# Spreading softmax weights over channels by a TensorE matrix instead of DMAs, and an earlier load of k, in a fused kernel of local attention and a state-space convolution

## The chip, the cores and the metric

The kernel runs on one core of a Trainium2 chip. The metric is device time in microseconds of one execution, and lower is better. The core has five engines that work side by side, each through its own instructions in order: TensorE (matmuls, PE in the profile), VectorE (DVE), ScalarE (ACT), GpSimd (POOL) and SyncE (SP), whose queue issues most DMAs. GpSimd's queue issues the rest. TensorE writes into PSUM, from where ScalarE moves results into on-chip memory ("evicts" them).

## The reference

Two independent halves share one output, side by side in the channels. All arrays are bf16, S = 2048 tokens, D = 576 channels.

```
# half A: 32 heads of 18 channels; a token looks at itself and 7 earlier ones, 2 apart
q, k, v = split(x @ wqkv)                                  # wqkv: 576 x 1728
logits[h, s, w] = sum_d q[h, s, d] * k[h, s - 2w, d] / sqrt(18)     # -1e9 where s - 2w < 0
attn = softmax(logits over w)
a = concat_heads(sum_w attn[h, s, w] * v[h, s - 2w, :]) @ wo        # wo: 576 x 576

# half B: a short convolution, a gate, a convolution as long as the sequence, a gate
k_shift[s, d] = sum_t k[s - 3 + t, d] * shift_k[d, 3 - t]           # 4 taps
kv = k_shift * v
y[s, d] = sum_{r <= s} kv[r, d] * ssm_k[d, s - r] + kv[s, d] * ssm_D[d]
b = q * y
out = concat([a, b], channels)
```

## The kernel before

**Order of work.** Nothing is issued where it is written. Each step is given to `Plan` by `op(engine, us, function, reads, writes, ...)`, with an engine letter (P TensorE, D VectorE, A ScalarE, G GpSimd, S SyncE), an assumed duration and the regions of buffers that it touches. `Plan.emit` sorts all steps once: for each engine it takes, among the steps that could begin earliest by the assumed durations, the one with the longest chain behind it (VectorE keeps close to the written order). The program then issues its instructions in that order, and every engine works through its own list strictly in order. So a changed step or a changed region can move instructions of other engines. PSUM is cut into four slots of two banks; a step with `opens` takes a slot and a later one with `closes` gives it back.

**Half A.** x is loaded by quarters of 512 tokens (`load_x`, `turn_x`) and turned by TensorE (`transpose_x`, `transpose_tail`) so that channels lie on partitions; quarters 2 and 3 are turned mostly by a transposing DMA. `project(comp, ct, jj)` computes q (comp 0), k (1) or v (2) for 128 channels and 1024 tokens: matmuls on L492 and L497, eviction on L516. `logits(hh)` takes one half hh of the tokens: VectorE multiplies q by four shifted views of k (L707, two product buffers), and TensorE adds the channels of each head by 0/1 matrices E into 32-row blocks j of 256 tokens (L717); ten products make a half, and after five of them ScalarE evicts a logits sum. `softmax(hh)` works on `attn[hh]`, 128 rows (4 token blocks of 32 heads) by 8 window positions by 256 tokens; its last step is the normalising multiply on L755.

To weigh v, the weights of a head must stand on all partitions of its channels. Each half has three chunks: c = 0 and c = 1 are two token blocks each with the 512 channels of ct 0 to 3, and c = 2 is all four blocks with the last 64 channels. `spread(n)` copies the 32 rows of a block to 64 partitions, each row to two neighbours, twice (four DMAs of 256 KB), into the buffer that `XB` names: chunks 0 and 3 share `tabk`, 1 and 5 share the start of `qk`, 4 has `qk` from 4096, 2 has `pv`. `weigh(n)` multiplies that buffer by shifted v on VectorE (L797, 128x4096; four products in a chunk c < 2, one in c = 2; three product buffers, `PB`), TensorE adds the eight window positions (L817, or L836 for c = 2), and ScalarE evicts into `pv` (L824). `output` multiplies by wo in sixteen groups (L869 and L872).

**Half B.** `taps(i)` computes k_shift and kv for a quarter of the tokens on VectorE (L569, L572, L579: eight instructions of 128x2304), from buffers that `load_k(i)` and `load_v(i)` fill. The kernel's shift weights come in as one row and are spread over the partitions by TensorE and ScalarE (`weight_rows`). The long convolution is done by tables of cosines and sines: `filter_spectrum` (ps_fk) for the filter and `x_spectrum` (ps_fx) for kv, both on L591 and L592 with evictions on L605; `partners` and `turn_filter` combine halves by accumulating DMAs from GpSimd's queue. In the last stage VectorE multiplies spectra (`products`, L941), TensorE adds them (`sums`, ps_z, L968) and transforms back (`inverse`, ps_inv, L1001), and `gate` multiplies by q and stores.

The early loads are given to the plan in this order:

```
    load_x(0)
    load_w(0, wv[:, 0], [r_w(0)])
    load_x(1)
    load_k(0)
    load_w(1, wv[:, 1], [r_w(1)])
    load_v(0)
    turn_x(0)
    load_k(1)
    load_v(1)
```

## Time and profile before

| | |
|---|---|
| median of 3 runs | 249.74 us (248.18 to 251.2) |
| the profiled execution | 249.37 us, of it 247.7 us span |
| busy: TensorE, VectorE | 203.3 us (82%), 201.0 us (81%) |
| busy: ScalarE, GpSimd | 136.2 us (55%), 45.4 us (18%) |
| moved by DMA | 40.74 MB, mean 164 GB/s |

The span is the time from the first to the last instruction of the profiled execution. Two engines are busy for four fifths of it, so an average names no bound; the stages have to be read one by one. A timeline row gives the start, the busy time, the engine, the line, and the operation with its output and inputs; a bracket says how long the engine had been idle before it and which work ended that wait. Some matmul records can be missing from a trace.

### The profile page before, as it was taken

The numbers are of one execution on the slowest core, as the hardware profiler recorded it, in microseconds if no ns is written. First come the engines' busy times: TensorE is split into PE (matmuls) and PEld (weight loads), VectorE is DVE, ScalarE is ACT, GpSimd is POOL, SyncE is SP. The second block draws the span as 40 slices with busy tenths as digits, with TensorE's granted clock in tenths as the row PEclk, the third lists the DMA queues.
The fourth block names the chain that finished last, engine by engine and source line by source line (L and its number), as shares of the span: only waits on it lengthen the run. The fifth ranks groups of instructions, "written<-read, shape, count | busy, mean of one in ns | idle before, by whom it ended". The sixth has DMA issues, their size and how long they took to land.

```text
span 247.7 us, 4427 instructions
## 1 busy us (share of the span) xinstructions
PE 203.3 (82%) x1838; PEld 102.9 (42%) x1845; DVE 201.0 (81%) x144; ACT 136.2 (55%) x186; POOL 45.4 (18%) x74
## 2 busy tenths in 40 slices
PE   4889989979999999996984399267499999956962
PEld 2453334323465533344642146023245566623532
DVE  7179999999986999999999300487999999999941
ACT  5843454696698963869991123015159756632351
POOL 7600030052404241174280000000001010010000
PEclk9999999999999999999999569957999999999798
DMA  6999969999913989999999999916301627473041
GB/s 208 333 278 293 372 125 283 221 220 160 127 24 44 156 107 173 188 230 218 194 194 199 204 180 198 228 70 171 118 0 50 145 46 195 146 181 108 3 145 46
DMA packets 36772, 40.74 MB, mean 164 GB/s; under 512 B 17264, under 2 KB 30448, under 8 KB 36752
## 3 DMA queue, kind: packets, MB, share of 16 engines
q1 hardware_dynamic: 26784, 26.81, 41.1%
q0 software_dynamic: 9968, 13.65, 35.0%
q8 instruction: 14, 0.23, 0.4%
q14 instruction: 6, 0.05, 0.1%
HBM read 13.11 MB, written 4.72 MB: 72 GB/s over the span
## 4 chain that ended last, share of the span: by engine, by line
PE 44%; DMA 17%; DVE 17%; issue 10%; ACT 7%; SPq 3%; POOL 0%; DVEq 0%; ACTq 0%; POOLq 0%
PE ps_proj L492 13%; PE ps_z L968 7%; PE ps_inv L1001 6%; DMA xw<-xw 6%; DVE big L707 5%; DMA pv<-big 4%; DMA tabk<-big 4%; PE ps_wo L869 4%; SPq L773 3%; DVE qk L941 3%; PE ps_fk L591 3%; DMA qk<-in_A_wo_dram 3%; PE ps_acc L817 2%; PE ps_proj L497 2%; DVE qk L797 2%
## 5 line engine op out<-in xcount | busy, mean ns | idle before, releaser
L492 PE MATMUL ps_proj<-xw 128*128 128x512 bf16 x185 | 46.4, 391 | 2.8 <-ACT qk L516 1.8
L707 DVE TENSOR_TENSOR big<-qk 128x4096 bf16<-128x4096 bf16 (+1 forms) x20 | 40.3, 2073 | 4.0 <-PE ps_log L717 3.4
L941 DVE TENSOR_TENSOR qk<-xw,Ks 128x3072 bf16<-128x3072 bf16 x18 | 30.9, 1750 | 0.0
L817 PE MATMUL ps_acc<-big,ident 64*64 64x512 bf16 x192 | 19.7, 442 | 12.9 <-DVE big L797 10.7
L492 PEld LDWEIGHTS <-xw 128*128 128x128 bf16 x192 | 17.5, 99 | 26.8 <-issue 9.5
L797 DVE TENSOR_TENSOR big<-tabk,big 128x4096 bf16<-128x4096 bf16 x6 | 13.6, 2287 | 16.9 <-DMA tabk<-big 15.8
L975 ACT ACTIVATE ab<-ps_z 128x768 bf16<-128x768 f32 x24 | 18.9, 808 | 13.3 <-PE ps_z L968 13.2
L824 ACT ACTIVATE pv<-ps_acc 128x1024 bf16<-128x1024 f32 x8 | 8.2, 1023 | 30.6 <-PE ps_acc L817 30.6
L516 ACT ACTIVATE qk<-ps_proj 128x1024 bf16<-128x1024 f32 x16 | 15.7, 1024 | 14.5 <-PE ps_proj L497 14.5
L869 PE MATMUL ps_wo<-qk,pv 128*128 128x288 bf16 x128 | 19.9, 302 | 1.1 <-ACT pv L824 1.1
L941 DVE TENSOR_TENSOR big<-xw,Ks 128x3072 bf16<-128x3072 bf16 x12 | 20.7, 1749 | 0.0
L605 ACT ACTIVATE Ks<-ps_fk 128x576 bf16<-128x576 f32 x32 | 18.8, 654 | 2.7 <-PE ps_fk L592 2.1
L817 PEld LDWEIGHTS <-ident 64*64 64x64 bf16 x256 | 9.3, 117 | 26.4 <-issue 16.3
L968 PE MATMUL ps_z<-qk,ident 64*64 64x384 bf16 x192 | 16.8, 339 | 3.5 <-DVE qk L941 3.4
L985 POOL DMA_DIRECT2D ab<-ab x3 | 3.6, 1196 | 85.6 <-ACT ab L975 85.6
L1001 PE MATMUL ps_inv<-ab,TI 128*128 128x288 bf16 (+2 forms) x128 | 18.2, 293 | 0.9 <-ACT ab L975 0.9
L605 ACT ACTIVATE xw<-ps_fx 128x576 bf16<-128x576 f32 x32 | 18.1, 679 | 0.9 <-PE ps_fx L592 0.9
L389 POOL DMA_DIRECT2D pv<-Ks x16 | 9.8, 616 | 44.8 <-DVE ab L572 24.3
L591 PE MATMUL ps_fk<-pv,tabk 128*128 128x384 bf16 x64 | 16.8, 328 | 0.2 <-ACT Ks L605 0.2
L572 DVE TENSOR_TENSOR ab<-ab,big 128x2304 bf16<-128x2304 bf16 x12 | 16.3, 1358 | 0.4
L591 PE MATMUL ps_fx<-ab,T 128*128 128x384 bf16 x64 | 16.6, 326 | 0.0
L569 DVE TENSOR_TENSOR big<-big 128x2304 bf16<-128x2304 bf16 x12 | 16.3, 1355 | 0.3
(120 smaller groups left out, 369.4 us busy)
## 6 DMA issues: line engine op xcount, KB each, us to landing
Ks<-Ks POOLq DMA_DIRECT2D x10, 576.0 KB, 10.1
qk<-big SPq DMA_DIRECT2D x12, 256.0 KB, 9.0
big<-in_B_k_dram SPq DMA_DIRECT2D x3, 1008.0 KB, 5.7
big<-in_B_v_dram SPq DMA_DIRECT2D x4, 576.0 KB, 10.0
pv<-Ks POOLq DMA_DIRECT2D x16, 144.0 KB, 8.0
xw<-xw POOLq DMA_DIRECT2D x4, 576.0 KB, 13.6
out_dram<-qk SPq DMA_DIRECT2D x8, 288.0 KB, 4.1
tabk<-big SPq DMA_DIRECT2D x8, 256.0 KB, 9.3
```

The lines of the kernel that those rows point to most:

```text
L492: nc.tensor.matmul(banks[key][:, jp, :], wq(kb, comp, 128 * ct, 128), xT(kb, 1024 * jj + 512 * jp, 512), start=(kb == 0), stop=False)
L569: nc.vector.tensor_tensor(o, kj[:, 3 - j:7 - j, :], skb[:, j, :].unsqueeze(1).to_broadcast([128, 4, D]), ALU.mult)
L591: nc.tensor.matmul(o[:, 0:2, :], w, rhs[:, 0:2, :], start=start, stop=stop, skip_group_check=True)
L605: nc.scalar.activation(dst(step), acc3(banks[key]), ACT.Copy, scale=scale * (1.0 if step else -2.0))
L707: nc.vector.tensor_tensor(view(prod, 0, [[m, 4], [1, m]]), view(t, oq, [[0, 4], [1, m]]), view(tk, oo + 2 + 8 * ug, [[2, 4], [1, m]]), ALU ...
L797: op("D", tt_us(4096), lambda: nc.vector.tensor_tensor(view(P, 0, [[2048, 2], [256, W], [1, 256]]), view(X, xo, [[2048, 2], [256, W], [1, ...
L817: nc.tensor.matmul(acc[64 * o:64 * o + 64, h, :], ident[64 * h:64 * h + 64, 64 * h:64 * h + 64], view(P, 256 * u, [[2048, 2], [1, 256]])[6 ...
L869: nc.tensor.matmul(ps[:, r, 0:HD], oT(hh, j + 2 * r, t)[:, o:o + 128], wo[:, t // 2, t % 2, HD * h:HD * h + HD], start=(t == 0), stop=False)
L941: op("D", 1.752, lambda: nc.vector.tensor_tensor(pr, view(xw, i * SPB + 4 * TH * t, [[4 * D, 2], [0, 2], [1, 4 * TH]]), view(Ks, (3 - j + ...
L968: nc.tensor.matmul(z[o:o + 64, h, 0:2 * TH], w[64 * h:64 * h + 64, 64 * h:64 * h + 64], pr[64 * h:64 * h + 64, part, cs, 2 * TH * q:2 * TH ...
L975: nc.scalar.activation(view(y_at(n, 1 - q, t, TH), 0, [[2 * D, 2], [D, 2], [1, TH]]), view(banks[key], 0, [[512, 2], [TH, 2], [1, TH]]), A ...
L1001: nc.tensor.matmul(ps[:, c, 0:w], TI[:, s // 2, s % 2, 2 * c + par, :], Yall[:, n % 2, par, s // 2, s % 2, c0:c0 + w], start=(s == 0), sto ...
```

## The change

Chunks with c < 2 (0, 1, 3 and 4) are no longer spread by DMAs. A new 0/1 matrix `rep` is built on GpSimd by eight selects: in each block of 32 rows, row h has ones in columns 2h, 2h + 1, 64 + 2h and 65 + 2h. For each quarter u of a chunk's 2048 columns, two matmuls of 32 rows take the two blocks into the two banks of a PSUM slot (`ps_rep`), and ScalarE evicts both at once (128x1024) into the same buffer that the DMAs filled. Chunks 2 and 5 keep their DMAs. k(0) is loaded second, w(0), x(1) and v(0) follow, and k(1) comes ahead of the transposing load. All four transposed pieces of x are evicted by ScalarE; VectorE had two. In `taps`, a multiply names to the plan only the four of seven rows of k that it reads.

```
+    rep = main.tile([128, 128], BF16, name="rep")
+    for j in range(4):
+        e = rep[32 * j:32 * j + 32, :].rearrange("p (e c) -> p e c", e=2)
+        nc.gpsimd.affine_select(e, ones128[32 * j:32 * j + 32, :].rearrange("p (e c) -> p e c", e=2),
+                                pattern=[[0, 2], [1, 64]], compare_op=ALU.is_ge, fill=0.0, base=0, channel_multiplier=-2)
+        nc.gpsimd.affine_select(e, e, pattern=[[0, 2], [-1, 64]], compare_op=ALU.is_ge, fill=0.0, base=1,
+                                channel_multiplier=2)
...
     load_x(0)
+    load_k(0)
     load_w(0, wv[:, 0], [r_w(0)])
     load_x(1)
-    load_k(0)
+    load_v(0)
     load_w(1, wv[:, 1], [r_w(1)])
-    load_v(0)
+    load_k(1)
     turn_x(0)
-    load_k(1)
     load_v(1)
...
-        transpose_x(0, kb, "A" if kb else "D")
+        transpose_x(0, kb, "A")
...
-        transpose_x(1, kb, "A" if kb else "D")
+        transpose_x(1, kb, "A")
...
-            op("D", 1.35, partial(mul, o, j), r=[rk, rw], w=[w], chain=True)
+            op("D", 1.35, partial(mul, o, j), r=[reg("big", o_kj[i % 2] + D * (3 - j), 4 * D), rw], w=[w], chain=True)
...
     def spread(n):
         hh, c = chunks[n]
         t, name, o = XB[n]
+        if c < 2:
+            for u in range(4):
+                key = ("rep", n, u)
+                own = reg("rep", 4 * n + u, 1)
+
+                def mm(u=u, key=key):
+                    ps = bank2(key, "ps_rep")
+                    for jj in range(2):
+                        j = 2 * c + jj
+                        nc.tensor.matmul(ps[:, jj, :], rep[32 * j:32 * j + 32, :],
+                                         attn[hh][32 * j:32 * j + 32, 2 * u:2 * u + 2, :], start=True, stop=True,
+                                         tile_position=(32 * j, 0))
+                op("P", 0.25, mm, r=[reg("big", AT[hh], 2048)], w=[own], opens=key, mode="s")
+                op("A", 1.02, lambda u=u, key=key: nc.scalar.activation(view(t, o + 512 * u, [[2048, 2], [1, 512]]),
+                                                                        banks[key][:], ACT.Copy),
+                   r=[own], w=[reg(name, o + 512 * u, 512), reg(name, o + 2048 + 512 * u, 512)], closes=key)
+            return
```

The plan also orders other work anew. Three places on ScalarE, whose list says what TensorE hands over and when, show it. In all, a row is a line of the kernel, the operation, its output and input, and how many stand in a row.

First, ScalarE at the first logits of half 0, before (L516 and L523 projections, L605 filter spectrum, L724 a logits sum, L748 the exponential):

```order
L523 ACTIVATE qk<-ps_proj 128x512 x2
L516 ACTIVATE big<-ps_proj 128x1024 x3
L605 ACTIVATE Ks<-ps_fk 128x3x192 x8
L724 ACTIVATE big<-ps_log 128x1024
L605 ACTIVATE Ks<-ps_fk 128x3x192 x18
L724 ACTIVATE big<-ps_log 128x1024
L605 ACTIVATE Ks<-ps_fk 128x3x192 x5
L748 ACTIVATE big<-big 128x2048
```

and now (the same operations, seven lines further down in the file):

```order
L530 ACTIVATE qk<-ps_proj 128x512 x2
L523 ACTIVATE big<-ps_proj 128x1024 x2
L612 ACTIVATE Ks<-ps_fk 128x3x192 x2
L523 ACTIVATE big<-ps_proj 128x1024
L612 ACTIVATE Ks<-ps_fk 128x3x192
L731 ACTIVATE big<-ps_log 128x1024
L612 ACTIVATE Ks<-ps_fk 128x3x192 x15
L731 ACTIVATE big<-ps_log 128x1024
L612 ACTIVATE Ks<-ps_fk 128x3x192 x5
L755 ACTIVATE big<-big 128x2048
```

Eight filter evictions, and the matmuls that feed them, moved from ahead of the second logits sum to behind it.

Second, ScalarE from the softmax of half 1 to chunk 2, before (L748 the exponential, L605 the spectrum of kv, L824 and L840 the weighed sums, L876 the output projection):

```order
L748 ACTIVATE big<-big 128x2048
L605 ACTIVATE xw<-ps_fx 128x3x192 x4
L824 ACTIVATE pv<-ps_acc 128x1024
L605 ACTIVATE xw<-ps_fx 128x3x192 x15
L824 ACTIVATE pv<-ps_acc 128x1024 x3
L840 ACTIVATE pv<-ps_acc 128x512
L876 ACTIVATE qk<-ps_wo 128x2x288 x4
```

and now (L789 is the new eviction, into the buffers of chunks 3 and 4; L849 and L865 are the weighed sums):

```order
L755 ACTIVATE big<-big 128x2048
L523 ACTIVATE big<-ps_proj 128x1024
L612 ACTIVATE xw<-ps_fx 128x3x192 x3
L849 ACTIVATE pv<-ps_acc 128x1024
L612 ACTIVATE xw<-ps_fx 128x3x192 x4
L530 ACTIVATE big<-ps_proj 128x512
L612 ACTIVATE xw<-ps_fx 128x3x192
L789 ACTIVATE tabk<-ps_rep 128x2x512 x4
L789 ACTIVATE qk<-ps_rep 128x2x512 x4
L849 ACTIVATE pv<-ps_acc 128x1024
L612 ACTIVATE xw<-ps_fx 128x3x192 x6
L849 ACTIVATE pv<-ps_acc 128x1024 x2
```

The spectrum of kv, which was nearly done here, is now split, and most of it stands behind the eight new evictions.

Third, ScalarE at the end of the weighing, before (L975 is the last stage's first sum):

```order
L876 ACTIVATE qk<-ps_wo 128x2x288 x4
L824 ACTIVATE pv<-ps_acc 128x1024
L876 ACTIVATE qk<-ps_wo 128x2x288 x4
L824 ACTIVATE pv<-ps_acc 128x1024 x3
L840 ACTIVATE pv<-ps_acc 128x512
L975 ACTIVATE ab<-ps_z 128x4x192
```

and now (L901 is the output projection, L1000 the last stage's first sum):

```order
L612 ACTIVATE xw<-ps_fx 128x3x192 x7
L849 ACTIVATE pv<-ps_acc 128x1024
L612 ACTIVATE xw<-ps_fx 128x3x192 x5
L849 ACTIVATE pv<-ps_acc 128x1024
L612 ACTIVATE xw<-ps_fx 128x3x192 x5
L849 ACTIVATE pv<-ps_acc 128x1024
L612 ACTIVATE xw<-ps_fx 128x3x192
L901 ACTIVATE qk<-ps_wo 128x2x288 x2
L849 ACTIVATE pv<-ps_acc 128x1024
L865 ACTIVATE pv<-ps_acc 128x512
L1000 ACTIVATE ab<-ps_z 128x4x192
```

Two groups of the output projection stand ahead of the last stage, where there were eight, and the other fourteen come inside it.

## Rows read from the trace of the kernel before

**Rows 1.** Stretches: length, busy PE PEld DVE ACT POOL (count), clock, DMA share, GB/s

```profile
0.00:14.27 14.27, 10.12 (x61) 5.79 (x62) 6.12 (x16) 9.11 (x12) 9.24 (x33) 1.00 0.88 277
...
96.50:109.78 13.28, 12.70 (x108) 5.29 (x107) 13.28 (x9) 8.66 (x13) 3.31 (x6) 1.00 1.03 200
109.78:128.90 19.12, 16.73 (x170) 10.80 (x170) 18.35 (x16) 17.59 (x28) 9.57 (x9) 1.00 1.14 207
128.90:158.20 29.30, 18.37 (x142) 9.31 (x139) 8.99 (x4) 6.27 (x8) 1.34 (x1) 0.83 1.07 196
158.20:181.20 23.00, 13.42 (x139) 6.09 (x139) 20.11 (x10) 5.61 (x8) 0.00 (x0) 0.78 0.43 128
181.20:216.00 34.80, 34.74 (x436) 20.49 (x440) 34.19 (x21) 24.43 (x36) 2.39 (x2) 1.00 0.40 101
216.00:231.00 15.00, 9.65 (x144) 5.55 (x140) 15.00 (x10) 4.89 (x7) 1.20 (x1) 0.93 0.51 126
```

**Rows 2.** VectorE's timeline: the taps, the logits' wait, the products, the last stage

```profile
14.27 1.35 DVE L569 TENSOR_TENSOR ab<-big 128x2304 bf16<-128x2304 bf16 x1
...
58.05 6.70 DVE L707 TENSOR_TENSOR big<-qk 128x4096 bf16<-128x4096 bf16 x3
...
76.56 7.83 DVE L707 TENSOR_TENSOR big<-qk 128x4096 bf16<-128x4096 bf16 x4 [2.61 <-PE ps_log L717]
...
128.91 2.29 DVE L797 TENSOR_TENSOR qk<-qk,big 128x4096 bf16<-128x4096 bf16 x1 [0.50 <-PE ps_acc L817]
...
140.09 2.29 DVE L797 TENSOR_TENSOR qk<-pv,big 128x4096 bf16<-128x4096 bf16 x1 [4.49 <-DMA pv<-big]
158.20 4.49 DVE L797 TENSOR_TENSOR big<-tabk,big 128x4096 bf16<-128x4096 bf16 x2 [15.81 <-DMA tabk<-big]
...
166.00 2.29 DVE L797 TENSOR_TENSOR big<-tabk,big 128x4096 bf16<-128x4096 bf16 x1 [1.10 <-PE ps_acc L817]
...
172.24 2.29 DVE L797 TENSOR_TENSOR qk<-qk,big 128x4096 bf16<-128x4096 bf16 x1 [1.75 <-PE ps_acc L817]
...
181.18 3.42 DVE L941 TENSOR_TENSOR qk<-xw,Ks 128x3072 bf16<-128x3072 bf16 x2
```

**Rows 3.** TensorE's timeline, single places

```profile
5.31 1.89 PE L455 MATMUL ps_x<-ident,Ks 128*128 128x128 bf16 x16 [0.87 <-DMA Ks<-in_A_x_dram]
...
9.18 3.59 PE L492 MATMUL ps_proj<-xw 128*128 128x512 bf16 x8
...
17.13 0.39 PE L497 MATMUL ps_proj<-xw 64*128 64x512 bf16 x2
...
37.47 0.42 PE L475 MATMUL ps_x<-ident,Ks 128*64 128x128 bf16 x8 [1.12 <-ACT TI L558]
37.83 1.90 PE L492 MATMUL ps_proj<-xw 128*128 128x512 bf16 x8
...
76.87 0.34 PE L591 MATMUL ps_fk<-pv,tabk 128*128 128x384 bf16 x1
...
77.12 0.33 PE L591 MATMUL ps_fk<-pv,tabk 128*128 128x384 bf16 x1
...
117.30 1.92 PE L817 MATMUL ps_acc<-big,ident 64*64 64x512 bf16 x32 [2.26 <-ACT xw L605]
...
148.97 1.15 PE L869 MATMUL ps_wo<-qk,pv 128*128 128x288 bf16 x8
...
150.28 1.15 PE L869 MATMUL ps_wo<-qk,pv 128*128 128x288 bf16 x8
```

**Rows 4.** SyncE's DMA queue: start and time of issue, two of the spreads

```profile
124.03 7.19 SPq L773 DMA_DIRECT2D pv<-big  x4
...
141.12 9.70 SPq L773 DMA_DIRECT2D tabk<-big  x4
```

**Rows 5.** DMA issues, part 6 of the page: count, KB each, median us to landing

```profile
pv<-big SPq DMA_DIRECT2D x4, 256.0 KB, 10.3
```

**Rows 6.** Part 5 of the page: busy, mean ns, idle before and what ended it

```profile
L516 ACT ACTIVATE qk<-ps_proj 128x1024 bf16<-128x1024 f32 x16 | 15.7, 1024 | 14.5 <-PE ps_proj L497 14.5
```

More of the change, by code (lines that the diff above doesn't have):

```diff
@@ L563, in taps @@
         kj, vt, kv = kjs[i % 2], vts[i % 2], ab[:, i]
-        rk, rv, rw, rt = (reg("big", o_kj[i % 2], 7 * D), reg("big", o_vt[i % 2], 4 * D), reg("big", o_skb, 4 * D),
+        rv, rw, rt = (reg("big", o_vt[i % 2], 4 * D), reg("big", o_skb, 4 * D),
                           reg("big", o_tB, 4 * D))
@@ L771, in fn @@
                 for e in range(2):
-                    j = 2 * c + jj if c < 2 else jj + 2 * e
+                    j = jj + 2 * e
                     nc.sync.dma_start(view(t, o + 2048 * jj, [[1, 2048]])[64 * e:64 * e + 64],
```

## The prediction

> **What bounds the kernel now.** I read the table of stretches first, then VectorE's timeline for the waits inside them, then TensorE and the DMA queue where those waits end. All times are of one execution: span 247.7 us, 249.37 us as timed, so 1.7 us lie outside the span; the median of the three runs shown is 249.74 us, so this execution stands for it within 0.2%.
>
> The table of stretches [rows 1] shows VectorE full from 96.50 to 128.9 us and again from 181.2 to 231 us. Between 128.9 and 158.2 it works 8.99 of 29.30 us, ScalarE 6.27, TensorE 18.37, while the DMA engines are at 1.07: there the kernel waits for copies. VectorE's timeline names them [rows 2]: the product of chunk 2 waits 4.49 us for the DMA into pv, that of chunk 3 waits 15.81 us for the DMA into tabk. Both are `spread`; the queue issues the one into tabk only at 141.12 [rows 4], behind the others, and all of them run beside the accumulating DMAs of `partners` and `turn_filter`. Three shorter waits, 0.50, 1.10 and 1.75 us, are for TensorE to give a product buffer back. Together that is 23.65 us of VectorE standing still between 109.78 and 181.18. Before 109.78 the one large wait is 2.61 us at 76.56, for a logits sum of TensorE. From 181.2 to 216 TensorE (34.74 of 34.80 us) and VectorE (34.19) are both full, so this last stage has no room for more TensorE work; from 216 on TensorE has 15.00 - 9.65 = 5.35 us free.
>
> **Early loads (first term).** k's three DMAs (by their shapes 128x2304, 112x1728 and 15x1728 in bf16: 1.03 MB) move ahead of the first weights (128x2304 and two of 64x576: 0.74 MB) and the second x. x(0) had landed when the first transposes ran at 5.31 [rows 3]; at 277 GB/s, the rate of the first stretch [rows 1], k is there 3.7 us later, at about 9.0. The other operand, the broadcast shift kernel, is ready earlier, since ScalarE's early work is not moved. So VectorE begins its convolution taps at 9.0 to 9.5 and not at 14.27 [rows 2], and as these run without a gap up to 58.05, they end at about 53. The two copies that VectorE gives to ScalarE stood in its idle time before the taps.
>
> That lead is not all kept, because the logits need TensorE. The weights now land after k: 9.0 + 0.74 MB at the same rate, 11.7, against projections that began at 9.18 [rows 3], so TensorE starts 2.5 us later. It gets 1.7 us of that back: the second inverse table is transposed in the idle time at the start, so its sixteen matmuls (eight of the size take 0.42 us, so 0.6 to 0.8; I take 0.6) and the wait of 1.12 us behind them at 37.47 [rows 3] vanish there. TensorE is 0.8 us late. But the written order changes in VectorE's favour: up to the second logits eviction ScalarE has 18 filter evictions and no longer 26. One drains four matmuls, a pair of them takes 0.25 us from start to start (76.87 to 77.12, [rows 3]), so 8 x 2 x 0.25 = 4.0 us of TensorE work go behind the logits instead of in front of them. The wait at 76.56 is for exactly these, so VectorE is 4.0 - 0.8 = 3.2 us earlier. **-3.2**; the ends are 0 (TensorE's late start is never made up) and -5.3 (the whole lead is kept). The later loads of k(1) and v(1) bear on no term: k(1) is now issued ahead of the transposing load, and v(1) is first needed after fifteen taps of 1.4 us, at about 30, some 10 us after its issue. The eight selects on GpSimd that build `rep` delay its later DMAs by a few us; what these bring is first read after 58.
>
> **Chunks 0 and 1 on TensorE and ScalarE (second term).** A pair of row-tiled matmuls of 512 columns takes 0.39 us (17.13, [rows 3]), so 16 pairs cost 6.2 us; if the two halves did not run side by side, 12.5. An eviction of 128x1024 takes 1.02 us [rows 6], 16 of them 16.4 us on ScalarE. The first eight run from VectorE's softmax 0 to the first product, where in the trace ScalarE is busy 8.66 of 13.28 us [rows 1]. The eight transform evictions that stood there go behind them, so 8.2 us fit. They hide behind the last logits products; they would stand on the path if all four PSUM slots were theirs when a logits sum wants one. **+0.5**, from 0 to +2.
>
> **The products (third term).** From 109.78 to 128.9 nothing but 0.5 us waited, so up to there the shift of -2.7 holds. Then 13 products are left at 2.2 us (two take 4.49, [rows 2]). Without any wait the last stage would begin at 181.18 - 23.65 - 2.7 = 154.8. What waits remain? Chunk 2 is still a DMA, issued behind softmax 1 at 124.03 [rows 4], now at 121.3. Before, its product started 16 us after; at the 10.3 us of one such copy [rows 5] with its three fellows issued in 2.5 us it would be 12.8, an estimate. It lands at 134 to 137; VectorE gets there at 133.5 (128.91 - 0.5 - 2.7, three products, and 1.2 us that the next sentences count): 2 us. Chunks 3 and 4 must first let chunk 0's last product read tabk; then eight evictions take 8.2 us, from about 123.5 to 131.7, long before chunk 3 is wanted at 138. But they fill ScalarE's queue and the PSUM slots, and the sum of chunk 1's first pair (1.9 us for 32 matmuls, as at 117.30 [rows 3]) comes late by about 1.2 us for the third buffer. Behind that ScalarE has 24 transform evictions between sums, and TensorE up to 28 transform matmuls (3.5 us) in front of a sum, where a pair of products takes 4.4 us: I count 0.9 us at chunk 3, and 1.1 us for what I cannot see. Together 5.2 of the 23.65 us: **-18.5**. The ends are -23.65 (no wait left) and -11 (the wait for chunk 2 is what it was, 4.5 us, and TensorE costs another 8).
>
> **The last stage (fourth term).** Before, eight of the sixteen groups of the output projection ran in the holes up to 181; now two do, and six go into the last stage. A group is 1.31 us (from 148.97 to the next at 150.28, [rows 3]), 7.9 us in all. By the order one of them comes before the point that was 216 us, five behind it, against 5.35 us free there: 1.3 + 6.6 - 5.35 = 2.5. The clock granted in that part was 0.93 [rows 1], after idle time, and fuller work could give some back; I count nothing. **+2.5**, from 0 to +7.9.
>
> **A rule against this.** What rows show: one pair of matmuls is 0.39 us and its eviction 1.02 [rows 3, 6]. The Trainium skill, TensorEngine Tiling (Array Packing), section PSUM Bottleneck, says that tiling speeds up TensorE but not the emptying of PSUM, which may then become the bottleneck. By that rule the evictions set the pace of the replication; it is the slower rival below, and the trace so far speaks against it only by ScalarE's idle time after 128.9.
>
> **Sum.** 249.37 - 3.2 + 0.5 - 18.5 + 2.5 = 230.7, against the median 231.
>
> **Rivals.**
> - The middle becomes TensorE's. From 96.50 to 181.2 it works 12.70 + 16.73 + 18.37 + 13.42 = 61.2 us [rows 1]. In the new order this stretch loses six output groups (7.9) and gains the 16 pairs (6.2 to 12.5) and 26 projection matmuls that the logits overtook (26 x 0.23 = 6.0; eight take 1.90 at 37.83, [rows 3]). That is 65.5 to 71.8 us, some of it at the low clock (0.83 and 0.78 there), which continuous work would shed, where the forecast leaves 66.7 us, from 96.50 - 3.2 to 181.18 - 2.7 - 18.5. At 71.8 plus 3 us of hand-overs the stage starts at 168: 239. For it: TensorE is then about as full as VectorE. Against: half of the work is independent of VectorE and fills gaps. Chance 0.2.
> - Nothing waits: all of 23.65 and 5.3 come, the last stage absorbs its groups: 249.37 - 28.95 = 220.4, with the 0.5 about 221. Chance 0.1.
> - The change does not do what it says: the copies into pv are late because of the accumulating DMAs, not of one another, and chunk 2 still comes at 140. Ten products (22 us) and 2 us of buffers follow: the stage starts at 164, and 249.37 - 17.2 + 2.5 = 234.7. It lies within the forecast's own spread; chance 0.15.
> - Slower: the sixteen evictions sit in ScalarE's strict order ahead of the sums, hold all four PSUM slots, and TensorE and then VectorE stop for each: 16 x (1.02 + 0.39) = 22.6 us on the path for 20.3 us of DMA waits removed, with all six groups added: 249.37 - 3.2 - 20.3 + 22.6 + 7.9 = 256.4. It decides from the point where each replication holds VectorE more than (20.3 + 3.2 - 7.9) / 16 = 1.0 us. For it: ScalarE is busy 17.59 of 19.12 us from 109.78 to 128.9 [rows 1]. Against: chunk 3's evictions end 6 us before their product. Chance 0.04.
>
> **How the numbers follow.** The forecast, 231, has 0.5, and 0.01 is left for what none of these names. The likeliest case alone reaches from 225 to 236 by the ends of its second and fourth terms and half the span of the third. Held 8 times in 10, the range takes in the TensorE rival and most of the no-wait one: 222 to 240. A difference under 1% is about what a measurement of this kernel cannot tell from none. Slower by over 1% is the last rival, 0.04; within 1% (247 to 252) needs a TensorE-bound middle and a lost lead together, 0.03; faster by over 1% is the rest, 0.93.
>
> **What would show it.** In the new profile: the first tap before 10 us; the first wait of VectorE among the logits shorter or gone at about 73; no DMA behind any wait but chunk 2's; VectorE's first spectrum product near 160; TensorE's free time after the first third of the last stage gone. The prediction is wrong if ScalarE runs unbroken between softmax 1 and chunk 3 with TensorE idle, if TensorE's clock falls in the middle, or if the last stage grows by more than 5 us over its 66.5.

## The result and the profile after

The changed kernel takes 228.34 us (median of 4 runs, 226.37 to 231.04) beside 248.96 us for the kernel before, measured with it (4 runs, 247.75 to 251.2): a ratio of 0.9136, with a 95% interval of 0.9026 to 0.9245. Here and below, ratios and their intervals leave out runs in a slower state, over 1.5% above the fastest of the same kernel, while medians and ranges count every run. The forecast was 231.0 in a range of 222 to 240. The profiled execution took 227.69 us, its span is 226.0 us, 21.7 less than before.

VectorE's timeline of the changed kernel, the rows that answer to [rows 2] (start, length, what it does, and in brackets the idle time before it and who ended it). Line numbers are 7 higher than before, behind `spread` 25:

```profile
9.00 1.36 DVE L576 TENSOR_TENSOR ab<-big 128x2304 bf16<-128x2304 bf16 x1 [3.13 <-DMA big<-in_B_k_dram]
...
30.06 1.36 DVE L586 TENSOR_TENSOR ab<-ab,big 128x2304 bf16<-128x2304 bf16 x1 [0.49 <-DMA big<-in_B_v_dram]
32.44 1.36 DVE L576 TENSOR_TENSOR ab<-big 128x2304 bf16<-128x2304 bf16 x1 [1.03 <-DMA big<-in_B_k_dram]
...
54.46 4.49 DVE L714 TENSOR_TENSOR big<-qk 128x4096 bf16<-128x4096 bf16 x2
61.09 5.81 DVE L714 TENSOR_TENSOR big<-qk 128x4096 bf16<-128x4096 bf16 x3 [2.13 <-PE ps_log L724]
...
72.88 7.83 DVE L714 TENSOR_TENSOR big<-qk 128x4096 bf16<-128x4096 bf16 x4 [0.73 <-PE ps_log L724]
...
106.99 1.23 DVE L714 TENSOR_TENSOR big<-qk 128x2048 bf16<-128x2048 bf16 x1 [1.45 <-PE ps_log L724]
...
109.20 2.29 DVE L822 TENSOR_TENSOR big<-tabk,big 128x4096 bf16<-128x4096 bf16 x1 [0.98 <-DMA qk<-in_A_wo_dram]
...
130.55 2.29 DVE L822 TENSOR_TENSOR qk<-qk,big 128x4096 bf16<-128x4096 bf16 x1 [2.50 <-PE ps_acc L842]
...
139.90 4.50 DVE L822 TENSOR_TENSOR big<-tabk,big 128x4096 bf16<-128x4096 bf16 x2 [0.45 <-ACT pv L849]
...
146.96 2.29 DVE L822 TENSOR_TENSOR big<-tabk,big 128x4096 bf16<-128x4096 bf16 x1 [0.36 <-PE ps_acc L842]
...
160.31 3.43 DVE L966 TENSOR_TENSOR qk<-xw,Ks 128x3072 bf16<-128x3072 bf16 x2
```

Read it against [rows 2]: the taps start 5.27 us earlier and end 3.6 us earlier (54.46, before 58.05), the logits' product that stood at 76.56 only 3.7, chunk 0's first product only 0.6 (109.20, before 109.78), and the last stage 20.9. The products wait for no DMA any more: of 23.65 us of standing still 3.31 are left. The wait at 109.20 is put down to a weight DMA; a logits sum of TensorE ended at 109.0 and VectorE went on at once, so I count it to that, like the 1.45 us before it. SyncE's queue, with [rows 4], issues chunk 2's copies in 3.07 us instead of 7.19:

```profile
123.73 3.07 SPq L798 DMA_DIRECT2D pv<-big  x4
...
137.28 4.91 SPq L798 DMA_DIRECT2D qk<-big  x4
```

The table of stretches of the changed kernel, with the columns of [rows 1] (the last row is the whole last stage):

```profile
93.16:109.20 16.04, 14.60 (x95) 4.03 (x95) 13.54 (x9) 11.43 (x13) 7.39 (x9) 0.79 1.16 177
109.20:130.55 21.35, 17.93 (x149) 8.44 (x150) 18.46 (x15) 15.53 (x19) 6.35 (x5) 0.92 0.64 119
130.55:144.30 13.75, 12.54 (x127) 7.26 (x128) 13.30 (x6) 12.28 (x18) 0.00 (x0) 1.00 1.07 198
144.30:160.31 16.01, 16.01 (x195) 9.17 (x196) 15.62 (x9) 12.48 (x20) 4.34 (x3) 1.00 0.82 161
...
160.31:195.10 34.79, 34.79 (x434) 20.20 (x430) 34.45 (x21) 23.99 (x35) 2.39 (x2) 1.00 0.53 125
195.10:210.10 15.00, 15.00 (x206) 8.63 (x201) 14.88 (x10) 8.40 (x13) 1.20 (x1) 1.00 0.60 162
210.10:226.00 15.90, 10.34 (x140) 6.30 (x128) 7.93 (x8) 6.56 (x10) 0.00 (x0) 1.00 0.28 94
160.31:226.00 65.69, 60.13 (x764) 35.12 (x756) 57.26 (x37) 38.95 (x56) 3.59 (x3) 1.00 0.49 126
```

TensorE (first figure behind the length) has no free time from 144 to 210 us. The last stage of the kernel before, as one row and its end behind [rows 1]:

```profile
231.00:247.70 16.70, 9.91 (x128) 6.10 (x120) 7.86 (x8) 5.57 (x8) 0.00 (x0) 0.91 0.21 72
181.18:247.70 66.52, 54.31 (x696) 32.14 (x696) 57.06 (x37) 34.92 (x50) 3.59 (x3) 0.96 0.38 99
```

So the stage holds 5.8 us more of busy TensorE and is 0.8 us shorter: TensorE's free time in it fell from 12.2 to 5.6 us.

What is left of waiting around the new replication, in TensorE's timeline of the changed kernel:

```profile
97.53 0.39 PE L785 MATMUL ps_rep<-big,rep 32*128 32x512 bf16 x2 [0.52 <-ACT tabk L789]
...
99.86 1.04 PE L724 MATMUL ps_log<-big,E 128*32 128x512 bf16 x8 [0.53 <-ACT tabk L789]
...
103.72 2.77 PE L499 MATMUL ps_proj<-xw 128*128 128x512 bf16 x6 [0.22 <-issue]
...
127.02 0.51 PE L842 MATMUL ps_acc<-qk,ident 64*64 64x512 bf16 x2 [2.27 <-ACT tabk L789]
```

Logits sums and product sums wait for ScalarE to empty replicated weights out of PSUM, by half a microsecond at 99.86 and by 2.27 at 127.02.

### The profile page after: what moved, and what is told of

It is laid out like the page before. It is cut to its first block, busy times and chain, and to the rows that moved or that the text cites. A ratio compares the mean times of both kernels' runs of the same rounds, so it can differ in the third digit from the quotient of the medians.

```text
span 226.0 us, 4485 instructions
## 1 busy us (share of the span) xinstructions
PE 202.5 (90%) x1869; PEld 100.8 (45%) x1877; DVE 200.7 (89%) x142; ACT 152.8 (68%) x204; POOL 51.6 (23%) x82
## 4 chain that ended last, share of the span: by engine, by line
PE 65%; DVE 10%; DMA 9%; ACT 8%; issue 4%; SPq 2%; ACTq 0%
PE ps_proj L499 13%; PE ps_z L993 10%; PE ps_wo L894 8%; PE ps_inv L1026 8%; PE ps_acc L842 6%; DMA big<-in_A_wqkv_dram 6%; PE ps_log L724 4%; PE ps_fx L598 4%; PE ps_fk L598 3%; DMA xw<-in_A_wqkv_dram 3%; DVE big L714 2%; DVE big L822 2%; ACT xw L679 2%; ACT tabk L789 2%; PE ps_fx L599 2%
## 5 line engine op out<-in xcount | busy, mean ns | idle before, releaser
L499 PE MATMUL ps_proj<-xw 128*128 128x512 bf16 x184 | 47.6, 400 | 3.7 <-ACT qk L523 2.1
L499 PEld LDWEIGHTS <-xw 128*128 128x128 bf16 x192 | 18.0, 102 | 29.0 <-issue 11.8
L1000 ACT ACTIVATE ab<-ps_z 128x768 bf16<-128x768 f32 x24 | 19.1, 808 | 6.7 <-PE ps_z L993 6.7
L523 ACT ACTIVATE qk<-ps_proj 128x1024 bf16<-128x1024 f32 x16 | 15.5, 1021 | 11.5 <-PE ps_proj L504 11.5
L1026 PE MATMUL ps_inv<-ab,TI 128*128 128x288 bf16 (+2 forms) x128 | 17.8, 287 | 0.9 <-ACT ab L1000 0.9
L894 PE MATMUL ps_wo<-qk,pv 128*128 128x288 bf16 x128 | 18.5, 288 | 0.0
L842 PE MATMUL ps_acc<-big,ident 64*64 64x512 bf16 x192 | 16.9, 398 | 1.5 <-ACT big L523 1.0
L598 PE MATMUL ps_fk<-pv,tabk 128*128 128x384 bf16 x64 | 18.0, 343 | 0.0
L599 PE MATMUL ps_fk<-pv,tabk 128*128 128x192 bf16 x64 | 16.3, 256 | 0.0
L901 ACT ACTIVATE qk<-ps_wo 128x576 bf16<-128x576 f32 x16 | 10.4, 650 | 8.3 <-PE ps_wo L897 7.7
L993 PE MATMUL ps_z<-qk,ident 64*64 64x384 bf16 x192 | 15.8, 329 | 0.0
L599 PE MATMUL ps_fx<-ab,T 128*128 128x192 bf16 x64 | 15.7, 246 | 0.0
L724 PE MATMUL ps_log<-big,E 128*32 128x512 bf16 x160 | 13.2, 413 | 2.5 <-DVE big L714 2.0
```

Of the source, the lines that this page charges most:

```text
L499: nc.tensor.matmul(banks[key][:, jp, :], wq(kb, comp, 128 * ct, 128), xT(kb, 1024 * jj + 512 * jp, 512), start=(kb == 0), stop=False)
L598: nc.tensor.matmul(o[:, 0:2, :], w, rhs[:, 0:2, :], start=start, stop=stop, skip_group_check=True)
L599: nc.tensor.matmul(o[:, 2, :], w, rhs[:, 2, :], start=start, stop=stop, skip_group_check=True)
L724: nc.tensor.matmul(banks[key][32 * j:32 * j + 32, uu, :], E[:], view(prod, (2 * uu * nj + jo) * 256, [[256 * nj, 2], [1, 256]]), start=(ct ...
L842: nc.tensor.matmul(acc[64 * o:64 * o + 64, h, :], ident[64 * h:64 * h + 64, 64 * h:64 * h + 64], view(P, 256 * u, [[2048, 2], [1, 256]])[6 ...
L894: nc.tensor.matmul(ps[:, r, 0:HD], oT(hh, j + 2 * r, t)[:, o:o + 128], wo[:, t // 2, t % 2, HD * h:HD * h + HD], start=(t == 0), stop=False)
```

## The experiments

The times of the kernel before in the three groups of runs were 248.83, 249.54 and 248.62 us. The groups are experiments 1 to 4, 5 to 8 and 9 to 12; the first two ran on one chip, the third on another.

**1. The loads without the replication.** All chunks go by DMA, the early loads stay changed.

```
-        if c < 2:
+        if False:
...
-                    j = jj + 2 * e
+                    j = 2 * c + jj if c < 2 else jj + 2 * e
```

> All six chunks are spread by DMAs as before; the early loads, ScalarE's four x evictions and the narrower reads in the taps stay. Theory (the copies set the middle, so a lead of 3 us in front of them is kept through the whole chain of copies): VectorE normalises softmax 0 some 3 us earlier than before and the time is 246 us. Rival (the lead is lost in waits for the logits and for the queue): 249 us, no change.

Measured: 251.13 us, but its four runs reach from 246.28, the theory's figure, to 254.72, so the time decides nothing. VectorE's timeline of an execution of 251.06 us:

```profile
138.97 2.29 DVE L822 TENSOR_TENSOR qk<-pv,big 128x4096 bf16<-128x4096 bf16 x1 [3.34 <-DMA pv<-big]
159.09 4.49 DVE L822 TENSOR_TENSOR big<-tabk,big 128x4096 bf16<-128x4096 bf16 x2 [17.83 <-DMA tabk<-big]
```

VectorE normalised softmax 0 some 3 us earlier, as the theory had it (93.64 us, before 96.50), but chunk 3's product starts at 159.09 where it started at 158.20 [rows 2]: in this execution the copies end no earlier, and the wait for them takes up the lead. Whether the loads alone gain anything, these runs leave open.

**2. The replication without the loads.** The load order, the two copies by VectorE and the taps' reads are those of the kernel before.

```
     load_x(0)
-    load_k(0)
     load_w(0, wv[:, 0], [r_w(0)])
     load_x(1)
-    load_v(0)
+    load_k(0)
     load_w(1, wv[:, 1], [r_w(1)])
-    load_k(1)
+    load_v(0)
     turn_x(0)
+    load_k(1)
     load_v(1)
```

> Loads, x evictions and tap reads as before; chunks 0, 1, 3 and 4 by TensorE and ScalarE. Theory (in the changed kernel VectorE came to chunk 0's first product only 0.6 us earlier than before, so the lead of the loads had been spent in waits for logits sums behind the replication): 229 us, within 1% of the changed kernel. Rival (the two parts add): 231.5 us, 3.2 us slower than the changed kernel.

Measured: 236.66 us, ratio 0.9513 (0.9447 to 0.958), 5 us above the slower of my two figures. VectorE has a wait among the taps as long as in neither other kernel; with it the DMA issues of the first 32 us (count, KB each, median us to landing):

```profile
29.20 1.36 DVE L576 TENSOR_TENSOR ab<-big 128x2304 bf16<-128x2304 bf16 x1 [4.75 <-DMA big<-in_B_k_dram]
...
tabk<-T POOLq DMA_DIRECT2D x4, 128.0 KB, 13.6
xw<-in_A_x_dram SPq DMA_TRANSPOSE x2, 13.3
```

In the kernel before the same two rows say 7.7 and 8.6 us. The suspect was GpSimd: `rep`'s eight selects stand ahead of its DMAs of the table and push these into the transposing load. Experiment 8 tests that.

**3 and 4. Chunk 1, and chunks 0 and 1, back on DMAs.** The diff is that of experiment 3; in experiment 4 the list is (3, 4). Both also have the line for `j` of experiment 1.

```
-        if c < 2:
+        if n in (0, 3, 4):
```

> Chunk 1 goes back to four DMAs, chunks 0, 3 and 4 stay on TensorE. Theory (the eight replications in a row hold PSUM slots, TensorE idles, its clock falls, and the logits sums come late: VectorE waited 1.45 and 0.98 us there): both waits go and the time is 226 us, 2 us faster than the changed kernel. Rival (these waits belong to the projections that the order puts there): 228.3 us, no change. If DMAs delay one another enough, chunk 1's or 2's product waits and it is 230 us or more.

> Chunks 0 and 1 by DMAs, only 3 and 4 on TensorE. Theory (what pays is that nothing stands behind chunk 2's copy in the queue at softmax 1): 226 to 228 us, as good as the changed kernel, with no wait for a DMA in front of the products of chunks 2 to 4. Rival (every copy taken off the DMA engines pays, since the accumulating DMAs of the filter fill them): chunk 2 waits about 4 us as before, and the time is 233 us.

Measured: 230.89 us (0.9268, 0.9207 to 0.9329) and 232.09 us (0.9319, 0.9249 to 0.9388). Neither is better than the whole change: the first overlaps its interval, the second lies just above it. VectorE in experiment 3:

```profile
107.52 2.29 DVE L822 TENSOR_TENSOR big<-tabk,big 128x4096 bf16<-128x4096 bf16 x1 [0.42 <-PE ps_log L724]
136.09 2.29 DVE L822 TENSOR_TENSOR qk<-pv,big 128x4096 bf16<-128x4096 bf16 x1 [3.32 <-DMA pv<-big]
```

and in experiment 4:

```profile
91.74 13.36 DVE L714 TENSOR_TENSOR big<-qk 128x4096 bf16<-128x4096 bf16 x7
108.65 2.29 DVE L822 TENSOR_TENSOR big<-tabk,big 128x4096 bf16<-128x4096 bf16 x1 [3.55 <-PE ps_fx L599]
```

With half of the early evictions gone, chunk 0's product comes 1.7 us earlier, and TensorE's granted clock there (93.16 to 107.50 us) is 1.00 and not 0.79. But chunk 2 is waited for again, and the time is that of the third expectation. The copy for chunk 1 does not stand in front of chunk 2's: it had landed at 118.94, and chunk 2's was issued at 121.84. What stands beside it is an accumulating DMA of kv's spectrum (`xw<-xw`, 576 KB), issued at 118.01; from 120 to 124 us the DMA engines are at 1.17. In the changed kernel the first of these is issued at 124.56, and from 120 to 124 us the DMA engines stand idle (0.00).

With all early evictions gone (experiment 4), the logits' seven products run without a gap: nothing of the loss at this place is left. The 3.55 us behind them are put down to ps_fx, but they are the copy into `tabk`: its fourth DMA, issued at 95.87, landed at 108.53, and VectorE's product began at 108.65. So a copy costs there what the evictions cost in the changed kernel. Chunk 2 is not waited for in experiment 4 (135.85), as the theory had it; the time is nearer to the rival's.

**5. Eight output groups of the last stage twice.** The first pass is overwritten by the second.

```
-                for t in range(4):
...
+                for rnd in range(2 if hh == 1 else 1):
+                    for t in range(4):
```

> The changed kernel with each of the eight output-projection groups of the second attention half issued twice (the second pass overwrites the first, so the output is the same): 8 x 1.31 = 10.5 us more of TensorE in the last stage, nothing else moved. Theory A (the last stage grew by 0.8 us less than nothing because TensorE had room there beside VectorE's unbroken products and a fuller TensorE kept its full clock): the groups go on fitting in part, VectorE's last product still starts about 53 us into the stage, and only the tail grows: +1 to +4 us, 229.5 to 232.5. Rival B (TensorE is the bound of the whole last stage, as its busy 34.8 of 34.8 and 15.0 of 15.0 us would have it, and the six groups moved there cost what they take): less the some 5 us free in the tail +5.5 us or more up to +10.5, 234 to 239, and VectorE shows waits for TensorE in the stage.

Measured: 238.01 us, ratio 0.9572 (0.9514 to 0.9631), 9.7 us over the changed kernel: the rival's figure. The last stage as one stretch:

```profile
159.10:235.30 76.20, 70.67 (x844) 41.50 (x836) 57.35 (x37) 38.94 (x56) 3.59 (x3) 1.00 0.42 109
```

Against the changed kernel's stage (65.69 and 60.13 us) 10.54 us more of TensorE make it 10.51 us longer, and VectorE now waits in it, up to 5.9 us at once, for sums that ScalarE evicts. In the changed kernel no further group fits.

**6. The replication matmuls behind the last read of their buffer.**

```
-                op("P", 0.25, mm, r=[reg("big", AT[hh], 2048)], w=[own], opens=key, mode="s")
+                op("P", 0.25, mm, r=[reg("big", AT[hh], 2048)],
+                   w=[reg(name, o + 512 * u, 512), reg(name, o + 2048 + 512 * u, 512), own], opens=key, mode="s")
```

> The changed kernel with the replication matmuls of a chunk ordered behind the last read of the buffer that they fill: TensorE no longer has replication pairs waiting in PSUM slots while ScalarE stands before chunk 0's last product, and transform evictions come ahead of chunk 3's. Theory (the waits left, 2.50 us at 130.55 and 2.4 us at 107 to 109, come from replication results that hold slots and ScalarE's place in front of the sums and the logits): VectorE's wait for the product buffer at 130.55 falls below 0.7 us, the two at 107 to 109 to below 1.2 us together, the last stage begins 2 to 3 us earlier, 225 to 227 us. Rival (TensorE's clock and its amount of work set these waits, not the slots): the same sum of waits within 1 us, at other places, 228 to 229. Third: chunk 3's own evictions now come late and its product waits for ScalarE by 1 us or more, 229 to 231.

Measured: 228.59 us, ratio 0.9178 (0.9112 to 0.9245), no difference from the changed kernel. The waits did move: 2.50 us at 130.55 became 1.29, the two before 109.20 together 1.13 instead of 2.43; but chunk 3 waits 1.14 us for its sum's eviction and three later products 0.85 to 1.39 us. The first logits wait of the profiled execution was also longer (3.77 us), though nothing in the order differs up to there.

**7 and 8. The matrix built behind the table's DMAs**, in the changed kernel (7) and in experiment 2's (8). `build_rep` holds the eight selects, which stood ahead of them.

```
+    op("G", 2.0, build_rep, r=[reg("tabk", 0, 1)], w=[reg("repm", 0, 1)])
...
-                op("P", 0.25, mm, r=[reg("big", AT[hh], 2048)], w=[own], opens=key, mode="s")
+                op("P", 0.25, mm, r=[reg("big", AT[hh], 2048), reg("repm", 0, 1)], w=[own], opens=key, mode="s")
```

> The changed kernel with GpSimd's eight selects of the replication matrix moved behind the four DMAs of the table (tabk<-T), which so go out about 4 to 7 us earlier, at about 8.7 instead of 15.5 us. Every other engine's order is the same. Theory (in the changed kernel k's second load is issued ahead of the transposing load, so that the delay of the table's DMAs is covered): no change beyond 0.7 us, 227.6 to 229.0. Rival (the delay holds up the early loads here too): the tap waits of 0.49 and 1.03 us and part of the wait of 2.13 us for the first logits sum go, 1 to 2 us, 226.3 to 227.3.

> The kernel with the replication alone (the loads in the old order), with GpSimd's selects of the replication matrix moved behind the table's four DMAs. Theory (in that kernel the selects pushed the table's DMAs into the time of the transposing load and of k's second load, and this cost the tap wait of 4.75 us for k's second part at 29.20): the wait is gone or under 0.5 us, and 236.66 falls by 4 to 5 us to about 232. Rival (the wait there is due to something else, such as ScalarE's or the queue's order): the wait stays at 4 us or more and the time within 1 us of 236.7.

Measured: 227.64 us (0.9164, 0.9111 to 0.9218) and 232.45 us (0.9319, 0.926 to 0.9378). Experiment 8's rows, to be held against those of experiment 2:

```profile
25.08 1.36 DVE L579 TENSOR_TENSOR ab<-big 128x2304 bf16<-128x2304 bf16 x1 [0.66 <-DMA big<-in_B_k_dram]
...
tabk<-T POOLq DMA_DIRECT2D x4, 128.0 KB, 7.9
xw<-in_A_x_dram SPq DMA_TRANSPOSE x2, 9.2
```

Only the selects moved, and the 4.75 us are 0.66: that is shown. In the changed kernel the same move is worth nothing that can be measured; that this is so because k's second part is issued there ahead of the transposing load was expected, and not tested by itself. The pair also prices the loads, with the x evictions and tap reads that go with them, once the copies are gone: 232.45 - 227.64 = 4.8 us by the medians, 3.9 by the ratios.

**9. Eight of ten matmuls left out of the same output groups** (the second half's share of one output is not computed).

```
-                for t in range(4):
+                for t in range(4 if hh == 0 else 0):
...
-                                     woh[64 * r:64 * r + 64, HD * h:HD * h + HD], start=False, stop=True,
+                                     woh[64 * r:64 * r + 64, HD * h:HD * h + HD], start=(hh == 1), stop=True,
```

> The changed kernel with eight of the ten matmuls left out of each of the eight output-projection groups of the second attention half (that half's share of one output is so not computed): some 9 us of TensorE work less in the last stage, the order unchanged. Theory (TensorE is the bound of the last stage of the changed kernel, after the doubled groups cost 9.2 us; in the kernel before, VectorE and idle tail were): the stage shortens until VectorE binds, which works 57.3 us in it: 3 to 6 us less, 222 to 225.5. Rival (the stage is VectorE's, with the moved groups just filling holes): -1 us or less, 227 to 229.

Measured: 226.86 us (223.66 to 230.13), ratio 0.9051 (0.8953 to 0.9148), an interval that overlaps the changed kernel's, so the time does not part the two. The last stage does:

```profile
160.88:225.60 64.72, 52.70 (x700) 30.13 (x692) 56.99 (x37) 38.58 (x56) 3.59 (x3) 0.99 0.50 128
```

7.4 us less of TensorE shorten it by 1.0, and VectorE has no wait over 0.4 us in it up to 218: the rival's reading, the opposite of experiment 5. Both hold: the stage stands at the corner. One group more costs its full length; taking groups away gives almost nothing, since VectorE's products then set it.

**10. Each eviction of replicated weights twice.**

```
-                op("A", 1.02, lambda u=u, key=key: nc.scalar.activation(view(t, o + 512 * u, [[2048, 2], [1, 512]]),
-                                                                        banks[key][:], ACT.Copy),
+                op("A", 1.02, lambda u=u, key=key: [nc.scalar.activation(view(t, o + 512 * u, [[2048, 2], [1, 512]]),
+                                                                         banks[key][:], ACT.Copy) for _ in range(2)],
```

> The changed kernel with each of the sixteen evictions of replicated weights issued twice on ScalarE: 16 x 1.02 = 16.3 us more of ScalarE, 8.2 of it between VectorE's softmax 0 and the products of chunk 1, 8.2 behind chunk 0's last product. Theory A (ScalarE has room, the forecast's view: only the hand-overs to TensorE's slots get later): +1 to +4 us, 229.5 to 232.5. Rival B (the slower rival of the prediction: the evictions stand in ScalarE's strict order ahead of the sums and the logits and hold the slots, so that each counts): +8 us or more, 236 to 245, with VectorE waiting for the product buffers at 130 and for the logits before 109.

Measured: 242.85 us, ratio 0.9741 (0.9662 to 0.9821), 14.5 us over the changed kernel. VectorE, then TensorE:

```profile
115.25 1.22 DVE L714 TENSOR_TENSOR big<-qk 128x2048 bf16<-128x2048 bf16 x1 [3.44 <-PE ps_log L724]
...
140.62 2.29 DVE L822 TENSOR_TENSOR qk<-qk,big 128x4096 bf16<-128x4096 bf16 x1 [3.52 <-PE ps_acc L842]
...
150.64 2.29 DVE L822 TENSOR_TENSOR big<-qk,big 128x4096 bf16<-128x4096 bf16 x1 [5.52 <-PE ps_acc L842]
...
106.22 1.04 PE L724 MATMUL ps_log<-big,E 128*32 128x512 bf16 x8 [1.36 <-ACT tabk L789]
...
137.13 0.47 PE L842 MATMUL ps_acc<-qk,ident 64*64 64x512 bf16 x2 [3.33 <-ACT tabk L789]
```

14.5 / 16 = 0.9 us for each extra eviction of 1.02 us: ScalarE's order ahead of logits and sums counts nearly in full, as rival B said. TensorE's granted clock from 93.20 to 176.00 was 0.86, so part of the 0.9 us may be the clock's; the run does not part them. The first set of sixteen had found most of ScalarE's free time; a second finds hardly any.

**11. Chunk 3 back on DMAs** (chunks 0, 1 and 4 on TensorE).

```
-        if c < 2:
+        if n in (0, 1, 4):
```

> The changed kernel with chunk 3 back on DMAs (chunks 0, 1 and 4 on TensorE): the copy into tabk is now second in the queue behind chunk 2's, with nothing else of the spreading in front. Theory (a copy is late by what stands in front of it and by the free buffer: tabk is free at about 117, the copy is issued behind softmax 1 and chunk 2's, takes about 10 us): chunk 3's product waits 0 to 4 us for it, 228 to 232. Rival (the copies are late because of the accumulating DMAs beside them, whatever their number): the wait for tabk stays above 8 us, 236 or more.

Measured: 241.56 us (0.9596, 0.9488 to 0.9705). My theory of 0 to 4 us of waiting fails, and the rival's figures came (over 8 us, 236 or more). VectorE and SyncE's queue:

```profile
145.74 4.49 DVE L822 TENSOR_TENSOR big<-tabk,big 128x4096 bf16<-128x4096 bf16 x2 [10.00 <-DMA tabk<-big]
...
122.20 3.06 SPq L798 DMA_DIRECT2D pv<-big  x4
...
126.12 9.78 SPq L798 DMA_DIRECT2D tabk<-big  x4
```

The first set of four copies is issued in 3.06 us, the second, right behind it, in 9.78, at a DMA share of 1.00 (122 to 146 us). So its place in the queue is not all: the DMA engines are full. From 95 to 175 us GpSimd's queue, which holds the accumulating DMAs, takes 62.4% of their time and SyncE's 26.6%; whether fewer accumulating DMAs would free the copy was not tried. Of the former 15.81 us, 10.00 come back with this one chunk. The last stage is longer too, 69.69 us at a clock of 0.94.

**12. Experiments 6 and 7 together.**

```
+    op("G", 2.0, build_rep, r=[reg("tabk", 0, 1)], w=[reg("repm", 0, 1)])
...
-                op("P", 0.25, mm, r=[reg("big", AT[hh], 2048)], w=[own], opens=key, mode="s")
+                op("P", 0.25, mm, r=[reg("big", AT[hh], 2048), reg("repm", 0, 1)],
+                   w=[reg(name, o + 512 * u, 512), reg(name, o + 2048 + 512 * u, 512), own], opens=key, mode="s")
```

> The changed kernel with both changes together: the selects of the replication matrix behind the table's DMAs, and the replication matmuls ordered behind the last read of their buffer. Theory (the two act in different places, the first before softmax 0, the second from 106 to 140): about 1 us below the changed kernel, 226 to 228. Rival (TensorE's last stage, full from its start to 210, sets the end whatever comes earlier by 1 us): within 0.7 us of it, 227.6 to 229.

Measured: 226.55 us (223.12 to 227.18), ratio 0.904 (0.8931 to 0.915). The median is 1.8 us lower, but the interval overlaps the changed kernel's (0.9026 to 0.9245): not shown to be faster. VectorE has no wait at the third product buffer any more (2.50 us at 130.55 in the changed kernel).

## Why the prediction was right, step by step

The four terms, measured as shifts of VectorE's timeline (they add up to the span's 21.7 us; from the end of softmax 0 at 93.16 us, before 96.50, to the first product at 109.20, before 109.78, to the last stage at 160.31, before 181.18):

| term | predicted | measured |
| --- | --- | --- |
| early loads | -3.2 | -3.3 |
| chunks 0 and 1 replicated | +0.5 | +2.8 |
| the products | -18.5 | -20.3 |
| the last stage | +2.5 | -0.8 |
| sum | -18.7 | -21.7 |

The forecast gained 3.0 us too little, and that it was not further off is in part luck: the second term cost 2.3 us more than forecast, while the third and the fourth came out 1.8 and 3.3 us better.

**Early loads.** The size is right, the way to it only in part. The taps begin at 9.00, but "these run without a gap" failed: they wait 0.49 and 1.03 us for the second load of v and the third of k, though the later loads were to bear on no term, and 3.6 of the 5.27 us are left at their end. The first logits sum takes 2.13 of these (61.09). The shorter wait that stood at 76.56 (0.73 us, before 2.61) gives most of that back, as forecast. The selects on GpSimd, which I called hidden, are hidden only in the new load order: in the old one they cost 4 to 5 us (experiments 2 and 8: 4.1 by the trace, 4.2 by the medians, 4.8 by the ratios). And the lead counts in full only with the copies gone (experiments 7 and 8), which the sum of terms had not said.

**Chunks 0 and 1.** The direction was right, the size too small by 2.3 us, more than the +2 of its upper end. The step that failed is "They hide behind the last logits products". That 8.2 us of evictions fit on ScalarE is so: in experiments 2 and 8, with the same eight evictions and the old load order, the logits' seven products run as before without a gap; in the changed kernel they do not. VectorE in the changed kernel, in experiment 2 and in experiment 8:

```profile
93.16 12.39 DVE L714 TENSOR_TENSOR big<-qk 128x4096 bf16<-128x4096 bf16 x6
...
100.84 13.37 DVE L714 TENSOR_TENSOR big<-qk 128x4096 bf16<-128x4096 bf16 x7
...
97.65 13.36 DVE L717 TENSOR_TENSOR big<-qk 128x4096 bf16<-128x4096 bf16 x7
```

The changed kernel differs in TensorE. It waited for evictions at 97.53 and 99.86 and was busy for 2.78 of the 4 us before 100. From 100 to 106.5 us its granted clock was then 0.50, the lower of its two levels, and projections, which the forecast had counted only in the TensorE rival, stand there in a row in front of a logits sum (103.72): six matmuls take 2.77 us, where eight took 1.90 at full clock [rows 3], which is 1.3 us more. VectorE's two waits are 2.43 us. Experiment 6, with as many evictions and a clock of 1.00 at this place, has 1.13; experiment 3, with half of them and 1.00, 0.69; experiment 4, with none and 1.00, none. So evictions and clock both have a part, and no run changed the clock alone. By the Trainium skill, TensorEngine Tiling (Array Packing), section PSUM Bottleneck, the emptying of PSUM may become the bottleneck once tiled matmuls have sped up TensorE. The trace agrees in part, with 0.5 and 2.27 us of TensorE's waits for it, and experiment 10 shows that the next evictions would pay 0.9 us each. The slower rival had the right mechanism and the wrong amount of room.

**The products.** I kept 5.2 of 23.65 us of waits; 3.3 are left. Chunk 2's copy, for which I kept 2 us, is not waited for: the queue issues it in 3.07 us, it has landed at 133.4, and VectorE arrives only at 137.2. The sum before the third buffer, for which I kept 1.2 us, costs 2.50: TensorE stood 2.27 us because `tabk`'s evictions, ahead of it in ScalarE's order, waited 1.68 us for chunk 0's last product, and the sum then ran at a granted clock of 0.53 (127 to 130 us), for 3.5 us from 127.02 to the end of its last matmuls, where an earlier one took 1.92:

```profile
117.68 1.92 PE L842 MATMUL ps_acc<-big,ident 64*64 64x512 bf16 x32 [0.96 <-ACT big L523]
...
129.89 0.63 PE L842 MATMUL ps_acc<-big,ident 64*64 64x512 bf16 x2
```

That chunk 3's copy was the dear one is shown by experiment 11. The rival by which chunk 2 still comes at 140 is out, but not what it rests on, the accumulating DMAs. Those of kv's spectrum stood beside chunk 2's copy before, and the new order on ScalarE issues them later. One of GpSimd's rows before, and the first one now:

```profile
118.62 1.43 POOL L611 DMA_DIRECT2D xw<-xw  x1 [4.67 <-ACT xw L605]
...
124.56 1.45 POOL L618 DMA_DIRECT2D xw<-xw  x1 [12.27 <-ACT xw L612]
```

From 120 to 124 us the DMA engines were at 1.21 before and are idle now, just ahead of chunk 2's copy; in experiment 3, where one stands at 118.01, that copy is late again. So the reordering helped beside the missing copies, and no run parts the two. It does not do it alone: in experiment 1 these DMAs also come later (from 118.86), and chunk 3 waits 17.83 us. The rival in which TensorE sets the middle did not come: its 65.5 to 71.8 us of work measured 61.1, in the 67.2 us from 93.16 to 160.31.

**The last stage.** Its start, 160.3, was forecast at 160; its length was not. The step that failed is "I count nothing" for the clock, and with it, less, "against 5.35 us free there". TensorE's busy time grew by 5.8 us, where six groups were counted as 7.9. At a granted clock of 1.00 instead of 0.93 and 0.91 the same transform sums and inverse transforms took 1.8 us less (busy time of L968 and L1001 before: 25.6 and 18.2 us; of L993 and L1026 after: 24.2 and 17.8). Free time fell by 6.7 us: the 5.35 counted, and 1.2 of the 6.8 behind 231, where the forecast had not looked (16.70 - 9.91 before, 15.90 - 10.34 in the last row but one now). So 5.8 - 6.7 = -0.8 stands for 7.9 - 5.35 = +2.5. Experiments 5 and 9 show that the stage is full with the six groups.

Of the signs that I had named against the forecast one did appear: the clock fell in the middle, to 0.50 from 100 to 106.5 us and again at 128. It has a part in the two waits that are left in front of 109.20 and at 130.55.

## What to carry to other kernels

When copies in a saturated queue hold the critical engine, a matmul that spreads and an eviction that stores can stand in for them, as long as ScalarE and PSUM have gaps at the right places: count the gaps between the waits that matter, not the idle sum of the stretch. A gain ahead of such a queue can be lost in the queue, so price edits together as well as one by one. Before a stage is called full, subtract the busy time of each engine to its very end, and put a row at full clock beside one at the low clock. When a wait is put down to work that the waiting instruction does not use, look for what landed at that moment.

## What the hardware showed that I had not expected

- Eight selects of 32x128 on GpSimd (0.29 us each in experiment 2) put four 128 KB DMAs off from 8.93 to 11.78 us. These then landed in 13.6 us instead of 7.9, the transposing load in 13.3 instead of 9.2, and the wait for a load behind it was 4.1 us longer (experiment 2 against 8).
- In the changed kernel the last three of the eight selects took 1.30 to 1.43 us each; they began at 9.08, when VectorE's taps had just begun (9.00). Whether the taps are the cause was not tested.
- The issue of four 256 KB copies took 3.06 us when the DMA engines had been nearly idle (a share of 0.15 from 120 to 124 us) and 9.78 right behind such a set (experiment 11).
- TensorE's granted clock was 0.79 in a stretch where it was busy 14.60 of 16.04 us, of it 0.50 from 100 to 106.5; matmuls of 512 columns in a row took 2.77 us for six, where eight had taken 1.90 [rows 3]. In experiment 2 it was busy for only 10.33 of 13.30 us at the same place (100.8 to 114.1) and kept 1.00.
